# Attention, soft expert layer and gated MLP in one kernel: new order of the expert layers, w2 read in 4 KB runs, new planner durations, transposes moved into layer 2

## The chip, the cores and the metric

The kernel runs on one core of a Trainium2 chip. The metric is the time of one execution in microseconds (us); three runs of the kernel before were timed, and one more execution was profiled.

The engines are called by the profile's names: PE (TensorE matmul), PEld (its weight loads), DVE (VectorE), ACT (ScalarE), POOL (GpSimd) and SP (the engine whose queue issues nearly all transfers).

## What is computed

All tensors are f32; there are 2304 tokens of 512 features.

```python
# 1. attention: 4 batches, 8 heads of 64, 576 positions, a causal window of 64
scores = q @ k.T / 8, kept where 0 <= i - j < 64
x = softmax(scores) @ v                                # (2304, 512)
# 2. soft mixture: 8 experts with 4 slots each
logits = x @ phi                                       # (2304, 32)
slot_input = softmax(logits, over tokens).T @ x        # (32, 512)
h = relu(slot_input[e] @ w1[e])                        # layer 1, w1 (8, 512, 1024)
slot_out[e] = h @ w2[e]                                # layer 2, w2 (8, 1024, 512)
x = softmax(logits, over slots) @ slot_out             # combine weights, (2304, 512)
# 3. MLP: w_in (512, 2048), w_out (2048, 512)
out = softplus(x @ w_in) @ w_out
```

## The kernel before

**Attention.** It goes over 18 tiles of 128 tokens. A tile's work is cut into named steps: `LQ`, `LK`, `LV` load q, k, v; `S` is the scores, `T` mask and row maximum (DVE), `M` the subtraction (POOL), `E` the exponential (ACT), `PT` and `PC` the transpose and its copy, `VD` the arrangement of v (two POOL copies, the second of which reads the new v tile), `PV` the product, `RI`/`XN` the division, `XT`/`XC` the transpose of x. After every four tiles, `LG` to `SA` compute logits and fold them into a running softmax over tokens. `LW` loads one 512 KB piece of w1, `W2` one of w2; all go through SP's queue. The last two tiles of logits go another way (`LD`, `LM`, `EX`, `F`, `DD`, `D2`, `P0`, `P1`), ending with the slot inputs (`SN`, `SI`, `SC`).

**The planner.** The order of the steps on each engine is not written by hand. `arrange` takes every step's cost on each engine that may do it, its dependencies and a due time, plays a greedy schedule, and returns the steps sorted by planned start. The kernel issues them so, and each engine executes its own in that order; the costs have no other effect. A loaded tile is taken to land `LANDS` = 2.0 us after its issue slot on Q (SP's queue). There are two plans: `steps_1` for attention, `steps` for the MLP. `TILE` is the planned time per attention tile.

**Layers 1 and 2.** These are written by hand. `emit_l1(grp)` does layer 1 of four experts (64 matmul records), `emit_relu` its relu, one half on ACT, one on DVE, into two buffers that both groups use. `emit_h1t` transposes the two halves on PE (L598), each followed by two DVE copies into `hTz` (L605). `emit_l2(j)` does layer 2 for pieces of w2; an odd j makes 8 matmul records, an even one none. `emit_nat` computes the logits of the last two tiles once more in the other orientation. The softmax over slots (L632 to L647, into `lnat` and `cc`) stands in the code ahead of `emit_relu(0)`.

**The MLP.** For each of 16 feature blocks f and each of five token groups of 4, 4, 4, 3 and 3 tiles, `H` computes the hidden block, `B`, `E` (ACT) and `G` (DVE) its softplus, `GH` and `GL` split it into two parts, `Y` adds three matmuls per tile (L858 to L860) to one of four PSUM banks, and `O` takes the sum out at the end of a slab. A slab is a range of f (`SLABS`); all groups pass through one slab before the next. Weights come as raw 64-bit data (`R`), four at a time at first, and are converted by four operations each (`C`), then split (`SH`, `SL`). Ahead of the first `H` stand: `SO`, `ST`, `SE` (the layer 2 result copied, transposed, copied), `CT` and `CE` (the combine weights `cc` transposed on PE and copied to `cT`), `WD`, `PC`, `PS` (w_in multiplied by the slot output). Where the plan leaves PE idle ahead of the first `Y`, `keep_warm` fills in matmuls without use (L140).

Of the kernel before, what the change touches and what calls it, by code (L numbers as in the profile page):

```python
# [24 lines left out]
SLABS = (0, 2, 5, 10, 16)  # L25
# [9 lines left out]
ENGINES = dict(GL="PD", GH="AD", SH="AD", SL="PD", WQ="AD", PC="A", O="AD", SO="AD", SE="A", CE="AD", C="AD")  # L35
# [6 lines left out]
TILE = 4.9  # L42
# [63 lines left out]
def block_kernel(ctx: ExitStack, tc: tile.TileContext, q, k, v, phi, w1, w2, w_in, w_out, cst, out):  # L106
# [79 lines left out]
    etd = sp1.tile([NS, 256], F32, name="etd")  # L186
# [193 lines left out]

    def do_lm(e, u):
# [7 lines left out]
    def do_ex(e, u):  # L389
        nc.scalar.activation(out=etd[:, 128 * u:128 * u + 128], in_=ps_t.pop(("ld", u))[0:NS, 0:128], func=AF.Exp, bias=gn[0:NS], accum_out=sd[:, u:u + 1])  # L390
# [37 lines left out]
    def emit_nat(t, bk):  # L428
        ps = bank(bk, "nat_ps")
        for kk in range(4):  # L430
            nc.tensor.matmul(ps[:, 0:NS], xt_t[t][:, 128 * kk:128 * kk + 128], phi_sb[:, kk, :], start=kk == 0, stop=kk == 3)
        nc.scalar.copy(lnat[:, t, :], ps[:, 0:NS])
# [8 lines left out]

    extra, wpc = [], []
# [9 lines left out]
    def emit_rinv():  # L452
        nc.vector.tensor_tensor(out=s_sum, in0=s_sum, in1=f_sb, op=ALU.mult)
        ps = bank(7, "r_ps")
        for u in range(2):
# [9 lines left out]
                D2=do_d2, P0=do_p0, P1=do_p1, SN=do_sn, SI=do_si, SC=do_sc, NA=do_na, CL=do_cl, W2=do_w2)  # L465
# [15 lines left out]
    for t in range(NT + 1):  # L481
        if t < NT:
            if t:
                step_1(("LQ", t), dict(Q=0.7), [("S", t - NQB)])
                step_1(("LK", t), dict(Q=0.7), [("S", t - NKB + 1)])
                step_1(("LV", t), dict(Q=0.7), [("PV", 2 * (t - NVB) + 1), ("VD", t - NVB + 1)])
# [42 lines left out]
    step_1(("P1",), dict(E=0.6), [("P0",), ("D2",), ("XN", 17)])
    for h in range(2):  # L530
        step_1(("SN", h), dict(A=0.36, D=0.4), [("P1",)])
        step_1(("SI", h), dict(E=0.3), [("SN", h), ("EX", 1), ("D2",)])
        step_1(("SC", h), dict(A=0.2, D=0.2), [("SI", h)], goal=110.0)
    step_1(("NA",), dict(E=0.6), [("XC", 16), ("XN", 17)], goal=111.0)
    for n, js in enumerate((range(NWC0), range(NWC0, NWC0 + NWC1))):
        step_1(("CL", n), dict(Q=0.01), [("S", 17), ("LW", N1 - 1)] if n == 0 else [("PV", 35), ("CL", 0), ("VD", 17)])
        for j in js:
            step_1(("W2", j), dict(Q=1.37), [("CL", n), ("W2", j - 1)])

    with tc.manual_schedule():  # L540
# [6 lines left out]
        nc.scalar.dma_start(out=phi_sb, in_=phi.rearrange("(k p) s -> p k s", p=128))  # L547
# [17 lines left out]
        def emit_l1(grp):  # L565
            ps = [bank(2 * grp + hh, "l1_ps") for hh in range(2)]
            l1_ps[grp] = ps
            for kt in range(4):
# [439 lines left out]
```

## Time and profile before

| | us |
|---|---|
| median of 3 runs (382.62 to 384.53) | 383.97 |
| the profiled execution, its own time | 381.92 |
| its span, first to last instruction | 380.1 |
| PE busy | 363.0 (95%) |
| DVE busy | 277.9 (73%) |
| ACT busy | 238.4 (63%) |
| POOL busy | 104.4 (27%) |

The span is counted from the first instruction; 1.8 us of the execution lie outside it. Busy time of PE counts a matmul to its modelled end, and matmuls are pipelined, so the distance between starts says more than the durations. A row of a timeline has a start, a duration, the engine and the line; what stands in brackets is idle time of the engine ahead of it, and what ended it.

### The profile page before, as it was taken

How to read it: one execution, taken by the hardware profiler on the slowest of the kernel's cores; microseconds unless marked ns; L12 is line 12 of the kernel's file. 1: busy time of each engine (PE TensorE's matmuls, PEld its weight loads, DVE VectorE, ACT ScalarE, POOL GpSimd, SP SyncE). 2: the span in 40 equal slices, each digit the busy share in tenths (PEclk: the TensorE clock that was granted, in tenths of full speed). 3: DMA queues.
4: the chain of work that ended last, by engine and by line, in shares of the span. 5: the costliest groups of instructions: out<-in, count | busy, mean ns of one | idle time of the engine just before them, and what ended most of it. 6: DMA issues, size and time to landing. Idle time of an engine off the chain costs nothing.

```text
span 380.1 us, 8149 instructions
## 1 busy us (share of the span) xinstructions
PE 363.0 (95%) x3013; PEld 268.9 (71%) x3013; DVE 277.9 (73%) x780; ACT 238.4 (63%) x467; POOL 104.4 (27%) x121
## 2 busy tenths in 40 slices
PE   7799999999898999998999999999999999999995
PEld 5588778786333285776887677878866888888884
DVE  1477777765144089999899989898899986767463
ACT  1467676753121089888858789466887794656760
POOL 2687787660011001021113421011324000002230
PEclk9999999999999999999999999999999999999999
DMA  8999999999999992341112433104010002112022
GB/s 290 365 322 399 401 393 399 397 403 382 381 376 387 377 353 92 114 164 55 56 57 62 153 119 110 41 17 148 17 57 2 1 20 92 55 58 83 28 85 83
DMA packets 35192, 70.27 MB, mean 185 GB/s; under 512 B 3280, under 2 KB 11472, under 8 KB 35152
## 3 DMA queue, kind: packets, MB, share of 16 engines
q1 hardware_dynamic: 34336, 69.03, 50.3%
q10 hardware_dynamic: 816, 0.72, 0.6%
q8 instruction: 24, 0.39, 0.4%
q14 instruction: 16, 0.13, 0.1%
HBM read 65.02 MB, written 4.72 MB: 183 GB/s over the span
## 4 chain that ended last, share of the span: by engine, by line
PE 75%; DVE 12%; ACT 5%; issue 4%; POOL 2%; DMA 1%; SPq 0%; DVEq 0%; POOLq 0%; ACTq 0%
PE y_ps L858 14%; PE y_ps L859 14%; PE y_ps L860 14%; PE x_ps L269 5%; PE pt_ps L251 5%; PE s_ps L224 5%; PE l_ps L613 3%; PE x_ps L829 2%; PE xt_ps L292 2%; DVE g L841 2%; PE l_ps L572 2%; PE h_ps L829 1%; ACT a L832 1%; DVE cv L699 1%; DMA vt<-v_d 1%
## 5 line engine op out<-in xcount | busy, mean ns | idle before, releaser
L858 PE MATMUL y_ps<-whi,gh 128*128 128x512 f32 x288 | 115.3, 400 | 1.3 <-DVE part L735 0.9
L859 PE MATMUL y_ps<-wlo,gh 128*128 128x512 f32 x288 | 114.2, 397 | 0.0
L860 PE MATMUL y_ps<-whi,gl 128*128 128x512 f32 x288 | 114.1, 396 | 0.1
L738 POOL TENSOR_TENSOR gl<-g,gh 128x384 fp32r<-128x384 f32 (+2 forms) x28 | 31.7, 1131 | 177.6 <-PE x_ps L829 62.0
L858 PEld LDWEIGHTS y_ps<-whi,gh 128*128 128x128 f32 x288 | 54.1, 188 | 17.3 <-issue 2.9
L860 PEld LDWEIGHTS y_ps<-whi,gl 128*128 128x128 f32 x288 | 54.1, 188 | 14.0 <-DVE gl L738 1.4
L859 PEld LDWEIGHTS y_ps<-wlo,gh 128*128 128x128 f32 x288 | 54.1, 188 | 11.6 <-DVE wlo L738 0.3
L837 ACT ACTIVATE a<-a 128x512 f32<-128x512 f32 (+2 forms) x81 | 47.4, 585 | 2.6
L836 ACT ACTIVATE a<-a 128x512 f32<-128x512 f32 (+2 forms) x81 | 47.3, 584 | 1.3
L235 DVE CUSTOM_DVE_ANT_0 sm<-s_ps,cst_sb 128x128 f32<-128x128 f32 x144 | 32.1, 287 | 20.9 <-PE s_ps L224 20.3
L832 ACT ACTIVATE a<-x_ps 128x512 f32<-128x512 f32 (+2 forms) x50 | 27.1, 546 | 25.5 <-PE x_ps L829 21.8
L242 POOL TENSOR_TENSOR sm<-mx,sm 128x512 f32<-128x512 f32 x36 | 37.0, 1035 | 13.6 <-ACT xt L195 6.9
L738 DVE TENSOR_TENSOR gl<-g,gh 128x512 fp32r<-128x512 f32 (+1 forms) x53 | 34.1, 646 | 2.9 <-ACT gh L735 1.6
L841 DVE SCALAR_TENSOR_TENSOR g<-x_ps,a 128x512 f32<-128x512 f32 (+2 forms) x50 | 31.2, 625 | 6.0 <-ACT a L832 2.1
L245 ACT ACTIVATE sm<-sm 128x512 f32<-128x512 f32 x36 | 22.7, 634 | 16.9 <-POOL sm L242 16.9
L735 DVE CAST gh<-g 128x512 fp32r<-128x512 f32 (+2 forms) x51 | 20.0, 393 | 13.2 <-PE y_ps L859 12.7
L869 DVE TENSOR_TENSOR part<-y_ps,part 128x512 f32<-128x512 f32 x36 | 24.6, 687 | 4.1 <-PE y_ps L860 3.2
L832 ACT ACTIVATE a<-h_ps 128x512 f32<-128x512 f32 (+1 forms) x31 | 17.0, 549 | 16.2 <-PE h_ps L829 16.0
L195 ACT COPY pt<-pt_ps 128x512 f32<-128x512 f32 x35 | 19.5, 586 | 11.2 <-PE pt_ps L251 11.0
L251 PE MATMUL pt_ps<-cst_sb,sm 128*128 128x128 f32 x144 | 22.2, 290 | 3.2 <-ACT sm L245 2.4
L224 PE MATMUL s_ps<-kr,qb 64*64 64x128 f32 x576 | 23.0, 301 | 1.9 <-DMA kr<-k_d 1.9
L224 PEld LDWEIGHTS s_ps<-kr,qb 64*64 64x64 f32 x576 | 18.0, 147 | 7.8 <-issue 5.2
(144 smaller groups left out, 551.9 us busy)
## 6 DMA issues: line engine op xcount, KB each, us to landing
w1t<-w_d SPq DMA_DIRECT2D x32, 512.0 KB, 7.7
w2t<-w_d SPq DMA_DIRECT2D x29, 512.0 KB, 10.2
wi<-w_in_d SPq DMA_DIRECT2D x16, 512.0 KB, 4.9
wo<-w_out_d SPq DMA_DIRECT2D x16, 512.0 KB, 4.0
vt<-v_d SPq DMA_DIRECT2D x18, 260.0 KB, 6.6
qb<-q_d SPq DMA_DIRECT2D x18, 256.0 KB, 6.1
out_d<-o SPq DMA_DIRECT2D x18, 256.0 KB, 2.0
kr<-k_d SPq DMA_DIRECT2D x17, 256.0 KB, 6.3
```

The costliest lines, as they stand in the source:

```text
L224: nc.tensor.matmul(s_ps[2 * t + a][64 * par:64 * par + 64, 128 * p:128 * p + 128], qb[t % NQB][rows, p, 64 * par:64 * par + 64], rhs, star ...
L235: nc.vector.tensor_tensor_reduce(out=sm[:, p], in0=ps[:, 128 * p:128 * p + 128], in1=mask, scale=-0.125, scalar=3.0e38, op0=ALU.add, op1=A ...
L242: nc.gpsimd.tensor_tensor(out=sm_t[i], in0=mb, in1=sm_t[i], op=ALU.subtract)
L251: nc.tensor.transpose(ps[:, 128 * p:128 * p + 128], sm[:, p], ident)
L738: eng[e].tensor_tensor(out=dst, in0=a, in1=b.bitcast(F32), op=ALU.subtract)
L832: nc.scalar.activation(out=st["a", i], in_=st["h", i], func=AF.Abs)
L836: nc.scalar.activation(out=a, in_=a, func=AF.Exp, scale=-1.0)
L837: nc.scalar.activation(out=a, in_=a, func=AF.Ln, bias=1.0)
L841: nc.vector.scalar_tensor_tensor(out=st["g", i], in0=st["h", i], scalar=0.0, in1=st["a", i], op0=ALU.max, op1=ALU.add)
L858: nc.tensor.matmul(y, st["gh", i][:, ts], hi, start=first, stop=False)
L859: nc.tensor.matmul(y, st["gh", i][:, ts], lo, start=False, stop=False)
L860: nc.tensor.matmul(y, st["gl", i][:, ts], hi, start=False, stop=last)
```

## The change

The diff does these things.

- **w2 runs.** In a piece of w2 each partition takes two neighbouring rows (one run of 4 KB) in place of rows 128 apart (two runs of 2 KB). Layer 1's hidden units are transposed with a step of two columns to match. Three of the 32 pieces are loaded into two half tiles each and keep 2 KB runs.
- **Logits of the last two tiles.** `emit_nat` goes (twice 8 matmul records and an ACT copy). In its place `LC` copies the logits beside the exponentials, `DD` transposes both together, and `NL` copies them into `lnat`.
- **Order of the layers.** After layer 1 of group 0: its relu, the first half of layer 1 of group 1, `emit_h1t(0)`, the second half, and then the softmax over slots, with `emit_relu(1)` in the middle of it. Eight pieces of layer 2, not six, stand ahead of `emit_h1t(1)`.
- **Combine weights.** `CT` and `CE` leave the MLP's plan. The 18 transposes and 5 copies stand between pieces of layer 2, on ACT and DVE in turn.
- **First slab.** Token group 0 has one block in its first slab and four in its second.
- **Planner.** Most costs are replaced: for instance `S` 1.15 to 1.05, `PV` 0.75 to 0.6, `VD` 1.5 to 1.25, transfers 0.7 to 0.67 and 1.37 to 1.31, `TILE` 4.9 to 4.6, `Y` 0.6425 to 0.7. `SE` may go on DVE as well.
- **phi** is laid out on the host so that each partition reads one run of 512 B in place of four of 128 B.

```diff
-SLABS = (0, 2, 5, 10, 16)
+SLABS = ((0, 1, 5, 10, 16),) + ((0, 2, 5, 10, 16),) * 4
-TILE = 4.9
+TILE = 4.6
...
-        src = w2[e, 256 * r:256 * r + 256, :].rearrange("(a p) f -> p a f", p=128)
+        src = w2[e, 256 * r:256 * r + 256, :].rearrange("(p a) f -> p a f", a=2)
...
+    def do_lc(e, u):
+        evac(e, etd[NS:2 * NS, 128 * u:128 * u + 128], ps_t["ld", u][NS:2 * NS, 0:128])
...
-            nc.tensor.transpose(ps_t["dd"][:, NS * u:NS * u + NS], etd[:, 128 * u:128 * u + 128], ident[0:NS, 0:NS])
+            nc.tensor.transpose(ps_t["dd"][:, 64 * u:64 * u + 64], etd[:, 128 * u:128 * u + 128], ident[0:64, 0:64])
...
+    def do_nl(e):
+        evac(e, lnat[:, 16:18, :], ps_t.pop("dd")[:, 0:128].rearrange("p (u s) -> p u s", u=2)[:, :, NS:2 * NS])
...
-    def do_na(e):
-        emit_nat(16, 4)
...
-                step_1(("LQ", t), dict(Q=0.7), [("S", t - NQB)])
+                step_1(("LQ", t), dict(Q=0.67), [("S", t - NQB)])
...
-                    step_1(("LW", j), dict(Q=1.37), [("LW", j - 1)], goal=100.0)
+                    step_1(("LW", j), dict(Q=1.31), [("LW", j - 1)], goal=100.0)
...
-                    nc.tensor.transpose(pst[:, 128 * f:128 * f + 128], h1[hh][:, 128 * f:128 * f + 128], ident)
+                    base = h1[hh][:, 256 * (f // 2) + f % 2:256 * (f // 2) + f % 2 + 1]
+                    rows = bass.AP(tensor=base.tensor, offset=base.offset, ap=[list(base.ap[0]), [2, 128]])
+                    nc.tensor.transpose(pst[:, 128 * f:128 * f + 128], rows, ident)
...
-        emit_nat(17, 5)
         emit_rinv()
+        emit_relu(0)
+        emit_l1(1, range(2))
+        emit_h1t(0)
+        emit_l1(1, range(2, 4))
...
         nc.vector.tensor_reduce(out=cm, in_=lnat, axis=AX.X, op=ALU.add)
+        emit_relu(1)
         nc.vector.tensor_scalar_add(cm, cm, 1e-9)
...
-        emit_relu(0)
-        emit_l1(1)
-        emit_h1t(0)
-        emit_relu(1)
-        for j in range(6):
+        for j in range(8):
             emit_l2(j)
         emit_h1t(1)
...
         for j in range(NWC, N2):
             emit_l2(j)
+            b, odd_j = divmod(j - NWC - 3, 2)
+            if not odd_j and 0 <= b < 5:
+                n = min(4, NT - 4 * b)
+                ps = bank((3, 0, 7)[b % 3], "c_ps")
+                for x in range(n):
+                    nc.tensor.transpose(ps[:, 128 * x:128 * x + 128], cc_t[b][:, x].rearrange("p a s -> p (a s)").bitcast(F32), ident)
+                (nc.vector.tensor_copy if b % 2 else nc.scalar.copy)(cT[:, 512 * b:512 * b + 128 * n], ps[:, 0:128 * n])
...
-        for a, b in zip(SLABS, SLABS[1:]):
+        for n in range(len(SLABS[0]) - 1):
             for g, nt in enumerate(GROUPS):
+                a, b = SLABS[g][n:n + 2]
                 for f in range(a, b):
...
-                step(("Y", i, j), dict(E=0.6425), deps, goal=goal)
+                step(("Y", i, j), dict(E=0.7), deps, goal=goal)
...
-        ("q_d", pairs(q)), ("k_d", pairs(k)), ("v_d", vh.reshape(NTOK, 520)), ("phi_d", inputs["moe_phi"]),
+        ("q_d", pairs(q)), ("k_d", pairs(k)), ("v_d", vh.reshape(NTOK, 520)), ("phi_d", inputs["moe_phi"].reshape(4, 128, NS).transpose(1, 0, 2)),
```

## Rows read from the trace of the kernel before

**Rows 1.** Busy time by stretch: start:end, length, engines' busy time (instructions), PEclk, DMA, GB/s.
```profile
30.00:50.00 20.00, 20.00 (x418) 16.39 (x414) 14.59 (x96) 14.44 (x30) 15.66 (x20) 1.00 1.04 398
...
122.10:133.40 11.30, 11.30 (x105) 3.28 (x104) 1.48 (x5) 0.00 (x0) 0.00 (x0) 1.00 1.06 379
...
150.00:180.00 30.00, 28.88 (x133) 21.66 (x134) 29.13 (x55) 25.38 (x52) 4.98 (x4) 1.00 0.32 106
```

**Rows 2.** PE in the MLP, timeline: Y matmuls 30 starts apart, and the last one.
```profile
150.12 0.39 PE L858 MATMUL y_ps<-whi,gh 128*128 128x512 f32 x1
...
157.11 0.34 PE L829 MATMUL h_ps<-cT,wst 128*128 128x384 f32 x1
...
375.92 0.40 PE L860 MATMUL y_ps<-whi,gl 128*128 128x512 f32 x1
```

**Rows 3.** PE's other matmuls in the MLP, groups by line: shapes xcount | busy us, mean ns | idle before.
```profile
L801 PE MATMUL wq_ps<-wit,soT 128*32 128x256 f32 x56 | 4.5, 391 | 0.9 <-DVE wit L700 0.9
...
L809 PE MATMUL wp_ps<-wq,cst_sb 128*128 128x256 f32 x14 | 4.2, 378 | 0.0
```

**Rows 4.** SP's queue near the end of attention, timeline.
```profile
71.71 2.36 SPq L146 DMA_DIRECT2D w1t<-w_d  x4
75.09 0.33 SPq L206 DMA_DIRECT2D vt<-v_d  x1
```

**Rows 5.** POOL at the last attention tile, timeline.
```profile
84.33 0.61 POOL L261 COPY vd<-vt 64x520 f32<-64x520 f32 x1 [1.55 <-DMA vt<-v_d]
```

**Rows 6.** DVE and ACT between attention and layer 1, timeline.
```profile
93.99 0.16 DVE L384 TENSOR_TENSOR gn<-gn,nm 128x1 f32<-128x1 f32 x1
94.64 0.18 ACT L432 COPY lnat<-x_ps 128x32 f32<-128x32 f32 x1 [2.31 <-PE x_ps L431]
94.73 0.30 ACT L387 ACTIVATE f<-negm,gn 128x1 f32<-128x1 f32 x1
```

**Rows 7.** PE in layers 1 and 2, timeline.
```profile
99.95 7.07 PE L572 MATMUL l_ps<-w1t,siT 128*32 128x512 f32 x64 [0.30 <-ACT siT L195]
106.96 1.08 PE L431 MATMUL x_ps<-phi_sb,xt 128*128 128x32 f32 x8
108.16 7.07 PE L572 MATMUL l_ps<-w1t,siT 128*32 128x512 f32 x64
117.15 0.66 PE L598 MATMUL x_ps<-cst_sb,s_acc 128*128 128x128 f32 x4 [1.33 <-DVE hTz L605]
117.74 2.78 PE L613 MATMUL l_ps<-w2t,hTz 128*32 128x512 f32 x24
121.55 0.66 PE L598 MATMUL x_ps<-cst_sb,s_acc 128*128 128x128 f32 x4 [0.44 <-DVE hTz L605]
122.13 11.37 PE L613 MATMUL l_ps<-w2t,hTz 128*32 128x512 f32 x104
```

**Rows 8.** DVE in the softmax over slots, its later part, timeline.
```profile
111.67 0.18 DVE L636 TENSOR_SCALAR cm<-cm 128x18 f32<-128x18 f32 x1
...
116.02 0.23 DVE L646 TENSOR_TENSOR cc<-lnat,cc 128x64 fp32r<-128x64 f32 x1
```

**Rows 9.** From layer 2 to the first Y, timeline.
```profile
132.14 0.43 DVE L694 TENSOR_SCALAR cv<-wi 128x512 f32<-128x512 f32 x1 [9.61 <-DMA wi<-w_in_d]
133.43 1.09 PE L747 MATMUL c_ps<-cst_sb,cc 128*128 128x128 f32 x8
137.53 0.27 ACT L735 CAST wst<-wp_ps 128x128 fp32r<-128x128 f32 x1
142.80 0.68 DVE L738 TENSOR_TENSOR wlo<-wot,whi 128x512 fp32r<-128x512 f32 x1
143.28 0.40 PE L858 MATMUL y_ps<-whi,gh 128*128 128x512 f32 x1
```

**Rows 10.** Transfers of raw w_in, by line: KB each, median us from issue to landing.
```profile
wi<-w_in_d SPq DMA_DIRECT2D x16, 512.0 KB, 4.9
```

More of the change, by code (lines that the diff above doesn't have):

```diff
@@ L185, in block_kernel @@
     negm = [sp1.tile([128, 1], F32, name=f"negm{i}") for i in range(2)]
-    etd = sp1.tile([NS, 256], F32, name="etd")
+    etd = sp1.tile([2 * NS, 256], F32, name="etd")
     sd = sp1.tile([NS, 2], F32, name="sd")
@@ L426, in do_sc @@
         evac(e, siT[h], ps_t.pop(("si", h))[:, 0:2 * NS])
[L428 to L432, printed above, removed]
-    def do_na(e):
-        emit_nat(16, 4)
+    extra, wpc = [], []
     def open_extra(st, bufs, side, first):
@@ L503, in block_kernel @@
             x = t - 1
-            in_ring(("XT", x), 0.55, ("XC", x), dict(A=0.58, D=0.69), [("XN", x)], [("LG", (x - XTB) // 4)])
+            in_ring(("XT", x), 0.54, ("XC", x), dict(A=0.58, D=0.69), [("XN", x)], [("LG", (x - XTB) // 4)])
             if x % 4 == 3:
                 b = x // 4
-                step_1(("LG", b), dict(E=1.15), [("XC", y) for y in range(x - 3, x + 1)] + [("SA", b - 1)])
+                step_1(("LG", b), dict(E=1.05), [("XC", y) for y in range(x - 3, x + 1)] + [("SA", b - 1)])
                 step_1(("LT", b), dict(A=0.27), [("LG", b)])
@@ L546, in block_kernel @@
         nc.scalar.dma_start(out=cst_sb, in_=cst)
-        nc.scalar.dma_start(out=phi_sb, in_=phi.rearrange("(k p) s -> p k s", p=128))
+        nc.scalar.dma_start(out=phi_sb, in_=phi)
         keep_warm(14, 7)
@@ L563, in block_kernel, with emit_l1 @@
         takers += [None] * (32 - len(takers))
[L565 to L568, printed above, removed]
+        def emit_l1(grp, kts=range(4)):
+            if grp not in l1_ps:
+                l1_ps[grp] = [bank(2 * grp + hh, "l1_ps") for hh in range(2)]
+            ps = l1_ps[grp]
+            for kt in kts:
                 for hh in range(2):
@@ L648, in block_kernel @@
             cc_t.append(cc)
-        emit_relu(0)
-        emit_l1(1)
-        emit_h1t(0)
-        emit_relu(1)
-        for j in range(6):
+        for j in range(8):
             emit_l2(j)
         emit_h1t(1)
-        for j in range(6, NWC):
+        for j in range(8, NWC):
             emit_l2(j)
@@ L741, in ncol @@
             return 128 * (items[i][5] - items[i][4])
-        def do_ct(e, b):
-            ps = st["ct", b] = bank((3, 0, 7)[b % 3], "c_ps")
-            for j in range(min(4, NT - 4 * b)):
-                nc.tensor.transpose(ps[:, 128 * j:128 * j + 128], cc_t[b][:, j].rearrange("p a s -> p (a s)").bitcast(F32), ident)
-        def do_ce(e, b):
-            n = 128 * min(4, NT - 4 * b)
-            copy(e, cT[:, 512 * b:512 * b + n], st["ct", b][:, 0:n])
         def do_so(e, h):
@@ L864, in do_o @@
             y = y_t.pop((g, j))
[L865 removed]
+            if f == SLABS[g][1] - 1:
                 copy(e, part[g, j], y)
@@ L892, in block_kernel @@
             step(("SE", h), dict(A=0.26, D=0.33), [("ST", h)])
-        for b in range(5):
-            n = 128 * min(4, NT - 4 * b)
-            step(("CT", b), dict(E=n * 0.00085), [("CE", b - 3)])
-            step(("CE", b), dict(A=0.09 + n * 0.00076, D=0.066 + n / 960), [("CT", b)])
         nb = 16 - NX
@@ L911, in block_kernel @@
                 m = 2 * j + u
-                step(("SH", m), dict(A=0.58, D=0.42), [("C", "wo", j, u, 3), ("SH", m - 1)])
-                step(("SL", m), dict(P=1.25, D=0.69), [("SH", m)])
+                step(("SH", m), dict(A=0.51, D=0.34), [("C", "wo", j, u, 3), ("SH", m - 1)])
+                step(("SL", m), dict(P=1.3, D=0.61), [("SH", m)])
             elif j == 0:
@@ L932, in block_kernel @@
             o = 128 * (start[g] + ta)
-            deps = [("PS", f // 2 + 1 if f > 1 else f), ("G", i - NA)] + [("CE", x) for x in range(o // 512, (o + n - 1) // 512 + 1)]
-            step(("H", i), dict(E=n / 2400 + 0.005), deps + ([held[b]] if b in held else []))
+            deps = [("PS", f // 2 + 1 if f > 1 else f), ("G", i - NA)]
+            step(("H", i), dict(E=n / 2200), deps + ([held[b]] if b in held else []))
             held[b] = ("G", i)
-            step(("B", i), dict(A=0.14 + n * 0.0008), [("H", i)])
-            step(("E", i), dict(A=0.35 + n * 0.0016), [("B", i)])
-            step(("G", i), dict(D=0.13 + n / 960), [("E", i), ("GL", i - NG)])
-            step(("GH", i), dict(A=0.15 + n * 0.00083, D=0.13 + n / 1920), [("G", i)] + [("Y", i - NH, j) for j in range(4)])
-            step(("GL", i), dict(P=n * 0.00238, D=0.13 + n / 960), [("GH", i)])
+            step(("B", i), dict(A=0.06 + n * 0.00085), [("H", i)])
+            step(("E", i), dict(A=0.26 + n * 0.00164), [("B", i)])
+            step(("G", i), dict(D=0.07 + n / 960), [("E", i), ("GL", i - NG)])
+            step(("GH", i), dict(A=0.08 + n * 0.00085, D=0.07 + n / 1920), [("G", i)] + [("Y", i - NH, j) for j in range(4)])
+            step(("GL", i), dict(P=0.15 + n * 0.0022, D=0.07 + n / 960), [("GH", i)])
             for j in range(ta, tb):
                 deps = [("GL", i), ("SL", f), ("Y", i, j - 1)]
-                if i == 0:
-                    deps += [("CE", x) for x in range(5)]
                 if first:
```

66 lines of the change are left out of this document (33 added, 33 removed).

## The prediction

> **What bounds the kernel now.** I read the busy time by stretch first. In attention PE is busy 20.00 of 20 us while the transfers run at 398 GB/s; in layer 2 PE is busy 11.30 of 11.30 us at 379 GB/s, with DVE and ACT nearly idle; early in the MLP (150 to 180) PE is busy 28.88 and DVE 29.13 of 30 us [rows 1]. So PE sets the pace throughout, transfers stand close behind it until layer 2 ends, and DVE stands close behind it in the first part of the MLP.
>
> Then the MLP's timeline. 30 matmuls take 157.11 - 150.12 = 6.99 us, 0.233 each [rows 2]. Y needs 288 x 3 = 864 of them, 201.3 us; H goes over 16 x 2304 columns, 72 matmuls of 512 columns, 16.8 us at the same pitch (an estimate). First Y to the end of the last is 376.32 - 143.28 = 233.0 us [rows 2, 9]. That leaves 14.9 us, of which the two other matmul groups take at most their busy 4.5 + 4.2 [rows 3]; pipelined like the rest I put them at 6. So PE stalls for some 9 us in the MLP (6 to 15 at the ends).
>
> Third, the places between stages, taken up below. The sum is made against the profiled execution, 381.92 us (span 380.1 and 1.8 around it); the median of the runs shown, 383.97, lies 2.05 above it, and I add that at the end.
>
> **Attention's order.** The last v tile is issued at 75.09, behind four w1 pieces from 71.71 [rows 4], and POOL waits 1.55 us for it [rows 5]. In POOL's order the last `M` is queued behind that copy; for `M` wait the last `E`, `PT`, `PV` and the whole end of the softmax. Why four pieces stand there: by the old costs a tile takes PE 1.15 + 2 x 0.55 + 2 x 0.75 + 0.55 + (1.15 + 0.35 + 0.75)/4 = 4.86, and the queue 3 x 0.7 + 2 x 1.37 = 4.84, so two w1 pieces fit in each tile. By the new ones PE takes 1.05 + 2 x 0.5 + 2 x 0.6 + 0.54 + (1.05 + 0.3 + 1.0)/4 = 4.38, and 3 x 0.67 leave 2.37 for w1, 1.8 pieces of 1.31. Fewer pieces should stand ahead of the last v; one less is 0.524 MB at 398 GB/s [rows 1], 1.3 us. The w1 pieces pushed back have until 99.95 [rows 7]. I take the wait as gone: -1.5. Bounds: the wait and one piece, -2.9; a wait of this size at another tile, +1.6. A new order of all other steps has no row and lies within these bounds only if no tile waits twice. phi's shorter runs: 64 KB at 398 GB/s is 0.16 us at most; 0.
>
> **Logits of the last two tiles.** `F` starts at 94.73 behind an ACT copy at 94.64 that waited 2.31 us for `emit_nat`; DVE had what `F` needs at 94.15 [rows 6]. Without that copy `F` can start 0.5 us sooner: -0.5 (0 if an `LC` copy comes to stand there). `LC` and `NL` are four copies of about 0.2 us like the one at 94.64, in ACT's idle 2.31 us; 0, and 0.8 if that cover is gone.
>
> **Layers 1 and 2.** Before, 99.95 to 133.43, 33.5 us [rows 7, 9]. After, in order: layer 1 of group 0, 7.0; `emit_rinv`, 0.3 (`emit_nat`'s 0.9, from 106.96, is gone); half of layer 1, 3.5; `emit_h1t(0)`, 1.7, its price when the second half waits 0.44 for DVE (it took 2.6 here, with a wait of 1.33); half of layer 1, 3.5; 32 records of layer 2 at 11.37/104 = 0.109, 3.5; `emit_h1t(1)`, 1.7; 96 records, 10.5; 18 transposes at 1.09/8, less the pipelined end, 2.3 [rows 7 to 9]. One wait moves: DVE does its half of `emit_relu(1)` (about 0.7, like the 512-column row at 142.80) only when layer 1 ends, then the rest of the softmax over slots, 116.25 - 111.67 = 4.6 [rows 8], and only then the copies for which the second transposes of `emit_h1t(1)` wait: 5.3 + 0.3 + hand-overs of 0.2 after layer 1's end. PE gets there at 3.5 + 0.66 and would wait 0.44 anyway, so it waits 1.1 more. Sum 35.1: +1.6. Bounds: no such wait, +0.5; transposes that read with a step of two columns have no row, and at twice the 0.66 of four they add 2.6 to the 16, so +4.2. I take the plain price, as all rows of PE's operands here are for plain reads. The five copies to `cT` lie under layer 2, where ACT shows 0.00 and DVE 1.48 of 11.3 us [rows 1]; without that cover, 5 x 0.68 = 3.4.
>
> **w2 in 4 KB runs.** 29 whole pieces are 15.2 MB: 40.1 us at the 379 GB/s of w2 in 2 KB runs, 38.2 at the 398 of the mixed loads of attention [rows 1]. The first raw weights, for which DVE waits until 132.14 [rows 9], should land 1.9 us sooner (0 at the other end, if SP's queue is held up elsewhere). In the sum it counts 0: layer 2 ends after that in either case. It is the cover for DVE's work at the MLP's start.
>
> A rule speaks against this part. The Trainium skill, "DMA: Bandwidth & Descriptors", section Bandwidth, says that for loads from HBM the HBM's share of about 358 GB/s for a core binds, not the run length. By that rule the raw weights land no sooner, and the MLP's start has to absorb up to 1.9 us. The trace does not agree: 398 GB/s in attention.
>
> **Start of the MLP.** From layer 2's end to the first `Y`: 143.28 - 133.43 = 9.85 us [rows 9]. PE's first eight `CT` transposes (1.09) stand ahead of `ST`; gone. From `PC` at 137.53 to `Y` at 143.28 pass 5.75 us, at whose end PE waits for `wlo`, started on DVE at 142.80 behind the conversion of block 1. With one block in group 0's first slab, block 1 is needed by the third item, not the second, so `wlo` need not wait for it. Eight short steps like `PC` (0.27) with hand-overs are an estimate of 3.3. So at best 9.85 - 1.1 - 2.45 = 6.3; I take 7.5, two thirds of the way, since DVE and ACT are contended there: -2.35 (bounds -3.5 and 0).
>
> **The first slab itself** adds no work: 18 `O` copies and ten items stand ahead of block 2 in both orders. Group 0's four copies come sooner, into a full DVE: 0, and 4 x 0.68 = 2.7 if all delay PE.
>
> **The MLP's planner.** `Y` at 0.7 is three times the measured 0.233; the old 0.6425 was too fast. Truer costs should remove some of the 9 us of stalls. But DVE has 0.9 us free in 30 [rows 1], and PE would start 2.6 us sooner against 1.9 us from the transfers. I take -1.5, nearer to nothing than to -9; at the other end stands the rival below.
>
> **Sum.** -1.5 - 0.5 + 1.6 - 2.35 - 1.5 = -4.25: 377.7 for an execution like the profiled one, 379.7 at the median.
>
> **Rivals.** *The planner does more* (0.15): two thirds of the 9 us go, -6 in place of -1.5, and the time is 375.2. For it: DVE and PE are both a little short of full. Against: nothing removes DVE work in the MLP but one copy.
>
> *DVE takes it back* (0.2): PE starts sooner, but each conversion is due when it was, so PE waits later; the -2.35 and the -1.5 vanish: -0.4, 383.6. It decides if the raw weights land no sooner. For it: 29.13 of 30 us; against it: 398 GB/s beside 379. (The rule of the Trainium skill's "DMA: Bandwidth & Descriptors" above would bring this rival about.)
>
> *Slower, by raw weights that the plan takes to be there* (0.12): the plan lets a conversion start 1.456 + 1.0 us after its slot in the queue, the transfers take 4.9 [rows 10]. With truer and tighter costs conversions are put earlier in the in-order queues of DVE and ACT; one that waits for its piece holds `G`, `GH` and `GL` behind it, and PE. Each costs up to 4.9 - 2.5 = 2.4 us; three of the 28 later pieces give +7.2 - 4.25, 386.9 at the median, and two already undo the gain. Against: before, the only wait of this kind is the harmless one until 132.14.
>
> **How the numbers follow.** The forecast has 0.53, its own range 377 to 382. I write down 379.7. A measurement of this kernel can tell about 0.5%, 1.9 us, from no change. Faster than 382.05: the forecast nearly whole, and the first rival, plus some of the second, 0.72; within, most of the second and the ends of others, 0.17; slower, 0.11. The range 375.5 to 385.0 takes in the second rival and leaves out the far halves of the first and third.
>
> **What would show it.** Right: POOL's wait for the last v gone and layer 1 starting near 98; layer 2 ending near 133 with `emit_h1t(1)` waiting 1.5 us; over 390 GB/s in layer 2 and DVE's first conversion near 130; the first `Y` near 140.7; stalls of PE in the MLP a little fewer. Wrong: a v or k wait at other tiles, stepped transposes slower than 0.66 for four, a first `Y` near 143, or stalls after 150 above 9 us.

## The result, and the profile after

The changed kernel takes 388.48 us at the median of four runs (386.66 to 390.27), the kernel before, beside it, 383.3 (381.15 to 384.53): a ratio of 1.0136, 95% interval 1.0091 to 1.0181. It is slower by 5.2 us, where 4.25 us faster was forecast. A few executions of a kernel run over 1.5% longer at a lower mean granted clock; medians are over all executions, and the ratios leave those few out. The profiled spans are 386.7 and 380.1, 6.6 apart, and the stages share that out:

| stage of the profiled execution, us | before | forecast | after |
|---|---|---|---|
| start to layer 1 | 99.95 | -2.0 | 98.39 (-1.56) |
| layers 1 and 2, with the transposes of the combine weights after | 33.5 | +1.6 | 39.3 (+5.8) |
| end of layer 2 to first `Y` | 9.85 | -2.35 | 7.71 (-2.1) |
| first `Y` to last `Y` | 232.6 | -1.5 | 237.0 (+4.4) |

Two terms failed: the layers by 4.2 us and the MLP by 5.9. PE's timeline through the layers of the changed kernel (start, duration, shape, count, idle time ahead) shows the first:

```profile
94.25 0.61 PE L401 MATMUL dd_ps<-cst_sb,etd 64*128 64x64 f32 x2 [1.38 <-ACT etd L393]
...
98.39 9.91 PE L572 MATMUL l_ps<-w1t,siT 128*32 128x512 f32 x64 [0.30 <-ACT siT L195]
...
113.30 0.75 PE L600 MATMUL x_ps<-cst_sb,s_acc 128*128 128x128 f32 x4 [0.44 <-DVE hTz L607]
...
123.17 0.75 PE L600 MATMUL x_ps<-cst_sb,s_acc 128*128 128x128 f32 x4 [1.44 <-DVE hTz L607]
...
128.28 0.66 PE L719 MATMUL c_ps<-cst_sb,cc 128*128 128x128 f32 x4
128.86 1.06 PE L615 MATMUL l_ps<-w2t,hTz 128*32 128x512 f32 x8
...
145.40 0.50 PE L858 MATMUL y_ps<-whi,gh 128*128 128x512 f32 x1
```

The same 64 matmuls of layer 1 that took 7.07 us before [rows 7] take 9.91. The windows of the changed kernel (columns as in [rows 1]) show the granted clock in this stretch:

```profile
93.00:94.00 1.00, 0.00 (x0) 0.00 (x0) 0.45 (x2) 0.45 (x2) 0.00 (x0) 1.00 1.05 418
97.00:98.00 1.00, 1.00 (x8) 0.95 (x7) 0.15 (x2) 0.21 (x1) 0.00 (x0) 0.67 1.03 412
98.00:104.00 6.00, 5.70 (x29) 1.36 (x32) 0.00 (x0) 0.21 (x1) 0.00 (x0) 0.50 0.98 357
104.00:105.00 1.00, 1.00 (x12) 0.24 (x8) 0.00 (x0) 0.00 (x0) 0.00 (x0) 0.92 0.96 322
```

PE does nothing from 93 to 94, and from late in 97 to 104 its granted clock is 0.50, the lower of its levels (1.2 in place of 2.4 GHz). Before, the clock was 1.00 in every microsecond from 90 to 102, and `emit_nat`'s eight matmuls stood (from 93.53 to 94.61) where the hole is now.

Ahead of that, POOL's wait for the last v, and then DVE at the MLP's start:

```profile
83.36 0.61 POOL L261 COPY vd<-vt 64x520 f32<-64x520 f32 x1 [1.09 <-DMA vt<-v_d]
```

```profile
133.72 0.69 DVE L720 CAST cT<-c_ps 128x512 fp32r<-128x512 f32 x1 [2.47 <-PE c_ps L719]
134.32 0.42 DVE L696 TENSOR_SCALAR cv<-wi 128x512 f32<-128x512 f32 x1
...
141.40 0.29 DVE L748 TENSOR_TENSOR wst<-wp_ps,wst 64x128 fp32r<-64x128 f32 x1 [3.12 <-ACT wst L745]
```

The wait of [rows 5] is 1.09 in place of 1.55. Three pieces of w1 stand ahead of the last v now, one fewer, but that v is issued only 0.52 sooner, at 74.57. DVE starts to convert at 134.32 (before 132.14, [rows 9]), since a copy to `cT` that waits for PE stands ahead in its queue, and then stands 3.12 us for `PC`.

In the MLP, groups by line with the idle time ahead of each and who ended it, between first and last `Y`: `H` in the kernel before, then `Y` and `H` in the changed one:

```profile
L829 PE MATMUL x_ps<-cT,wst 128*128 128x512 f32 (+1 forms) x47 | 18.7, 399 | 0.7 <-DVE g L841 0.3 <-ACT a L832 0.3
L829 PE MATMUL h_ps<-cT,wst 128*128 128x512 f32 (+1 forms) x30 | 11.3, 377 | 0.4 <-DVE g L841 0.4
```

```profile
L858 PE MATMUL y_ps<-whi,gh 128*128 128x512 f32 x288 | 116.6, 405 | 0.9 <-ACT part L745 0.4 <-DVE part L869 0.2
...
L829 PE MATMUL x_ps<-cT,wst 128*128 128x512 f32 (+1 forms) x48 | 19.2, 400 | 3.7 <-DVE g L841 3.0 <-DVE wst L748 0.6
L829 PE MATMUL h_ps<-cT,wst 128*128 128x512 f32 (+1 forms) x30 | 11.2, 373 | 0.7 <-DVE wst L748 0.7
```

PE stood 1.1 us in all ahead of `H` (L829) before, 0.7 of it for `G` on DVE; now it stands 4.4, of which 3.0 for `G`. `GL` on DVE and on POOL shows what is new there, first of the kernel before, then of the changed one (count, shortest/median/longest ns, from when to when):

```profile
L738 DVE TENSOR_TENSOR gl<-g,gh x53: 546/683/694, 144.3 to 371.0; 128x512 fp32r<-128x512 f32 x37, 128x384 fp32r<-128x384 f32 x16
L738 POOL TENSOR_TENSOR gl<-g,gh x28: 453/1027/1514, 142.0 to 369.0; 128x384 fp32r<-128x384 f32 x17, 128x512 fp32r<-128x512 f32 x10, 128x128 fp32r<-128x128 f32 x1
```

```profile
L748 DVE TENSOR_TENSOR gl<-g,gh x73: 537/682/693, 148.4 to 377.5; 128x512 fp32r<-128x512 f32 x46, 128x384 fp32r<-128x384 f32 x27
L748 POOL TENSOR_TENSOR gl<-g,gh x8: 459/1030/1417, 145.5 to 270.5; 128x384 fp32r<-128x384 f32 x6, 128x128 fp32r<-128x128 f32 x1, 128x512 fp32r<-128x512 f32 x1
```

With the new costs (`GL` dearer on POOL, cheaper on DVE) 20 `GL` steps went from POOL to DVE.

### The profile page after: what moved, and what is told of

It reads as the page before. It is cut to its first block, busy times and chain, and to the rows that moved or that the text cites. A ratio compares the mean times of both kernels' runs of the same rounds, so it can differ in the third digit from the quotient of the medians.

```text
span 386.7 us, 8083 instructions
## 1 busy us (share of the span) xinstructions
PE 366.4 (95%) x3004; PEld 266.8 (69%) x3004; DVE 284.5 (74%) x794; ACT 244.6 (63%) x474; POOL 81.4 (21%) x101
## 4 chain that ended last, share of the span: by engine, by line
PE 62%; DVE 21%; ACT 9%; issue 5%; DMA 1%; POOL 1%; SPq 0%; DVEq 0%; ACTq 0%; POOLq 0%
PE y_ps L858 10%; PE y_ps L860 10%; PE y_ps L859 10%; PE x_ps L269 5%; PE pt_ps L251 5%; PE l_ps L572 4%; PE s_ps L224 4%; DVE g L841 4%; DVE gl L748 3%; PE l_ps L615 3%; DVE part L869 2%; PE xt_ps L292 2%; DVE cv L701 2%; ACT a L836 2%; PE x_ps L829 2%
## 5 line engine op out<-in xcount | busy, mean ns | idle before, releaser
L858 PE MATMUL y_ps<-whi,gh 128*128 128x512 f32 x288 | 116.6, 405 | 0.9 <-ACT part L745 0.4
L748 DVE TENSOR_TENSOR gl<-g,gh 128x512 fp32r<-128x512 f32 (+1 forms) x73 | 46.5, 636 | 2.9 <-DVE gh L745 0.5
L195 ACT COPY pt<-pt_ps 128x512 f32<-128x512 f32 x36 | 20.4, 588 | 10.7 <-PE pt_ps L251 10.6
L748 POOL TENSOR_TENSOR gl<-g,gh 128x384 fp32r<-128x384 f32 (+2 forms) x8 | 8.6, 1076 | 87.0 <-PE y_ps L860 31.1
L745 DVE CAST gh<-g 128x512 fp32r<-128x512 f32 (+2 forms) x52 | 21.5, 413 | 6.1 <-PE y_ps L859 3.8
L841 DVE SCALAR_TENSOR_TENSOR g<-h_ps,a 128x512 f32<-128x512 f32 (+1 forms) x31 | 19.6, 631 | 8.1 <-ACT a L837 7.6
L748 POOL TENSOR_TENSOR wlo<-wot,whi 128x512 fp32r<-128x512 f32 x7 | 9.7, 1380 | 74.5 <-ACT whi L745 74.4
```

What stands on the lines that cost most here:

```text
L748: eng[e].tensor_tensor(out=dst, in0=a, in1=b.bitcast(F32), op=ALU.subtract)
L841: nc.vector.scalar_tensor_tensor(out=st["g", i], in0=st["h", i], scalar=0.0, in1=st["a", i], op0=ALU.max, op1=ALU.add)
L858: nc.tensor.matmul(y, st["gh", i][:, ts], hi, start=first, stop=False)
```

## The experiments

**The clock.** *Filler matmuls.* Theory: the hole that `emit_nat` left ahead of `DD` brings the lower clock. Twelve matmuls without use fill it.

```diff
         logits(ps_t["ld", u], [16 + u] * 4)
+        if u:
+            keep_warm(12, 4)
```

> The changed kernel with twelve matmuls without use put on PE right behind the last logits, where emit_nat stood before. Theory 'clock': without emit_nat PE stands idle from 92.87 to 94.25 in the changed kernel, and its granted clock is 0.50 from about 98 to 104, so layer 1 of group 0 takes 9.84 us and not 7.0; with the gap filled the clock stays at 1.00, layer 1 takes 7.1, and the span shrinks by 2.5 to 3 us, from 386.7 to about 384. Rival 'operands': layer 1 is slow because of what it reads while 4 KB writes land in the same memory; then it stays near 9.8 and the time is that of the changed kernel.

Measured: 386.7 us, ratio 1.0092 [1.0067, 1.0117]. The window and layer 1 of this kernel:

```profile
98.00:104.00 6.00, 5.70 (x57) 2.00 (x60) 0.00 (x0) 0.43 (x2) 0.99 (x2) 1.00 1.04 392
```

```profile
98.80 7.07 PE L574 MATMUL l_ps<-w1t,siT 128*32 128x512 f32 x64 [0.30 <-ACT siT L195]
```

Layer 1 is back at 7.07 and the span is 2.4 us shorter; the stretch of the `Y`s stays at 237.1. So the clock is one loss, and the MLP another. The same filler in the kernel with the whole MLP plan undone (both are shown below) takes the median from 382.01 to 380.76.

*The kernel before without `emit_nat(16)`.* The logits of tile 16 in this orientation are zeros here, so that part is left out.

```diff
-        emit_nat(16, 4)
+        nc.gpsimd.memset(lnat[:, 16, :], 0.0)
```

> The kernel before with the logits of tile 16 in the second orientation left out: eight matmuls of emit_nat and their ACT copy go, POOL writes zeros in their place, so the combine weights of that tile are uniform and not the reference's. Theory 'clock': PE now idles from about 93.5 to 95.4, the granted clock falls to 0.50 for some 6 us behind it, layer 1 of group 0 takes 9 to 10 us in place of 7.07, and the time rises by 2 us although work was taken away. Rival 'operands' (or no tie to the gap): layer 1 stays at 7.07 and the time falls by 0.5.

Measured: 382.1 us over ten runs (380.72 to 388.14), ratio 0.9982 [0.9946, 1.0017]: the 2 us that the theory named can't be seen. Its profile, of the slowest of the ten, has 10.2 us at half clock from 99.1, but half clock before the hole as well, from 88.9 to 92.3. Over all profiles: of the seven kernels with the changed attention and no filler, all spend 8.4 to 9.8 us on layer 1 of group 0; of the five with filler, two take 7.0 and three 8.3 to 8.7; of the seven with the attention of the kernel before, six have the full clock there, and one (the DVE copies, below) has not. The mean clocks of single executions say the same: in all 40 of the seven kernels without filler it is at most 0.995, while 7 of the 48 with filler and 3 of the ten without `emit_nat(16)` have 0.996 or more. So the hole makes the lower clock likelier; it doesn't force it, and the lower clock comes without it too.

**Single parts of the MLP undone.** First the old costs back in the changed kernel (core of the edit; the others are the diff of the change, read backwards):

```diff
-            step(("GL", i), dict(P=0.15 + n * 0.0022, D=0.07 + n / 960), [("GH", i)])
+            step(("GL", i), dict(P=n * 0.00238, D=0.13 + n / 960), [("GH", i)])
...
-                step(("Y", i, j), dict(E=0.7), deps, goal=goal)
-                goal += 0.7
+                step(("Y", i, j), dict(E=0.6425), deps, goal=goal)
+                goal += 0.6425
```

> The changed kernel with all costs of the MLP's plan as they were before (Y 0.6425, GL on POOL 0.00238 a column, and so on); order of the layers, slab, w2 and attention's plan stay changed. Theory 'planner': the new costs made the plan leave GL on DVE (73 subtractions there in place of 53, 8 on POOL in place of 28), DVE is over 96% busy from 180 to 260, and PE waits for g; with the old costs POOL has about 31 of them again, the stretch from first to last Y goes from 237.4 back to about 233, and the time falls by 4 us. Rival 'slab': the one-block slab of group 0 is what costs; then the stretch stays at 237 and the time does not move.

Measured: 389.56 us, 1.0175 [1.0131, 1.0218]; first to last `Y` 237.2. Then the old slab:

```diff
-SLABS = ((0, 1, 5, 10, 16),) + ((0, 2, 5, 10, 16),) * 4
+SLABS = ((0, 2, 5, 10, 16),) * 5
```

> The changed kernel with the first slab of group 0 of two blocks, as before. Theory 'planner': the slab is not the cause; the stretch from first to last Y stays above 236 and first Y comes later, near 146 to 147, so the time is the same or 1 us longer. Rival 'slab': the early evacuation of group 0 is what costs; then the stretch falls to about 233 and the time by 2 to 4 us.

Measured: 389.44 us, 1.0176 [1.0137, 1.0214]; 236.9. And both at once:

> The changed kernel with both the old costs of the MLP's plan and the old first slab, so that of its MLP only CT and CE are missing from the plan of before. Theory 'head of queue': PS(0) again stands on DVE ahead of the last conversions of the first blocks, DVE idles for some 3 us for it, and the stretch from first to last Y stays near 237 us. Rival 'costs and slab together': either alone is enough to spoil the order; with both undone the stretch returns to about 233 and the time falls by 4 us.

Measured: 394.21 us, 1.0265 [1.0193, 1.0338]; 239.0, the worst so far. With the old costs `GL` is back on POOL (50 on DVE, and 52 with the old slab too), and the stretch is no shorter. Taken alone, these three seem to clear both parts. That reading was wrong: single parts in the kernel before, below, lose each by itself.

**DVE's wait at the MLP's start.** The plan is told that layer 2 ends 2.7 us later after DVE is free:

```diff
-FREE = dict(E=2.64, A=0.28, D=2.18, P=2.48, Q=0.1)
+FREE = dict(E=5.34, A=0.28, D=2.18, P=2.48, Q=0.1)
...
-L2_END, GOAL, SLACK, NEAR = 2.74, 4.0, 0.65, 0.1
+L2_END, GOAL, SLACK, NEAR = 5.44, 6.70, 0.65, 0.1
```

> The changed kernel whose MLP plan is told that PE and the end of layer 2 come 2.7 us later against DVE (FREE E 5.34, L2_END 5.44, GOAL 6.7), as its trace shows: DVE is done with the copies to cT at 134.3, layer 2 ends at 137.7, 3.3 us later, where the plan has 0.56. In the changed kernel DVE stands idle for 3.1 us (138.3 to 141.4) with PS(0) at the head of its queue. Theory 'head of queue': with this plan one w_out conversion, SH(0) and SL(0), 1.6 us of work, stand ahead of PS(0), the idle time shrinks to about 1.5, DVE's later work comes 1.6 us sooner, and the time falls by 1 to 2 us. Rival 'chance of the greedy order': each change of the plan's numbers gives another order with a stretch of 236 to 238 us from first to last Y; the time does not move.

Measured: 387.02 us, 1.009 [1.005, 1.0129]; DVE's wait for `PC` is 1.17 in place of 3.12, the stretch 235.7. A second kernel has the filler, all copies to `cT` on ACT, and the plan told 6.0 us:

> The changed kernel with the twelve matmuls behind the last logits, all five copies to cT on ACT, and the MLP's plan told that layer 2 ends 6 us later against DVE. DVE can then begin with the raw weights when they land, about 130.5, not at 134.3, and has more conversions ahead of PS(0). Theories 'clock' and 'DVE' together: 2.4 us from the clock, 1 to 3 us from DVE's earlier start, time 383 to 385, level with the kernel before. Rival 'chance of the greedy order': 386.5 as with the twelve matmuls alone.

Measured: 385.66 us, 1.0056 [1.0018, 1.0094]; 235.6. So the start numbers that the plan was left with may cost some 1.4 of the 4.4; that it isn't just another order is not shown, since a `Y` of 0.65 moves the stretch by 0.8 below. The converse, nine useless copies (4.11 us) on DVE after the first conversion of the kernel before:

```diff
             st["c", kind, j, u][k](e)
+            if (kind, j, u, k) == ("wi", 0, 0, 3):
+                for _ in range(9):
+                    nc.vector.tensor_copy(cst_sb[:, 128:640], cst_sb[:, 128:640])
```

> The kernel before with nine copies of a 512-column tile onto itself put on DVE behind the first converted w_in block, 9 x 0.34 = 3.1 us of work without use; the output is unchanged. Theory 'DVE': time that DVE loses at the MLP's start is not made good before DVE has slack, so most of it, 2 to 3 us, comes back in the time, part as a later first Y, part as a longer stretch after it. Rival 'PE': PE sets the pace of the MLP, and only the delay of the first Y counts, at most 1 us or so, with the stretch after it at 233 or shorter.

Measured: 389.9 us, 1.0159 [1.007, 1.0249]. In its profile layer 1 starts 4.8 us later and takes 9.7 us, mostly at half clock; both lie ahead of the edit, so the total says little. The stages do: end of layer 2 to first `Y` 11.7 instead of 9.85, first to last `Y` 232.6, as before. Of the 4.1 us that DVE loses at the start 1.9 come back as a later first `Y`, none in the stretch, which needs another cause.

**The whole MLP plan undone.** `CT` and `CE` are steps of the plan again, with old costs, old slab and `SE` on ACT; what stands ahead stays changed:

```diff
-SLABS = ((0, 1, 5, 10, 16),) + ((0, 2, 5, 10, 16),) * 4
+SLABS = ((0, 2, 5, 10, 16),) * 5
...
+        for b in range(5):
+            n = 128 * min(4, NT - 4 * b)
+            step(("CT", b), dict(E=n * 0.00085), [("CE", b - 3)])
+            step(("CE", b), dict(A=0.09 + n * 0.00076, D=0.066 + n / 960), [("CT", b)])
```

> The changed kernel with its whole MLP plan set back: old planner costs, old slabs, transposes and copies of the combine weights as steps of the plan again. Attention, layers 1 and 2 and the 4 KB loads of w2 stay changed. Theory A, the order of the MLP alone loses the 4.4 us between first and last Y: the stretch returns to 232.6 us (232 to 233.5), layer 2 is about 1 us shorter than in the changed kernel, first Y comes about 9.9 us after it instead of 7.7, and the profiled span is about 386.7 - 4.4 + 2.1 - 1.0 = 383.4, or 380.6 if layer 1 also gets its full clock. Theory B, something ahead of the MLP (the loads that land sooner, DVE's late start) makes the stretch longer: it stays at 236 to 237.

Measured: 382.01 us, 0.9991 [0.9956, 1.0026]; stretch 232.4, end of layer 2 to first `Y` 9.85, span 379.8. The order of the MLP alone carries its loss. `H` in this kernel:

```profile
L832 PE MATMUL x_ps<-cT,wst 128*128 128x512 f32 (+1 forms) x46 | 18.2, 396 | 0.7 <-DVE g L844 0.3 <-ACT a L835 0.2
L832 PE MATMUL h_ps<-cT,wst 128*128 128x512 f32 (+1 forms) x30 | 11.4, 379 | 0.4 <-DVE g L844 0.4
```

Only `CT` and `CE` back in the plan, new costs and slab kept:

> The changed kernel with only the transposes and copies of the combine weights moved back from layer 2 to the MLP's plan; new costs and slabs stay. Theory A1, their move is what unsettles the order: the stretch from first to last Y is 232 to 234. Theory A2, the new costs or the slab do it, each alone being enough: it stays at 236 to 238 us. In both layer 2 with its transposes is 13.8 - 1.0 = about 12.8 us, and first Y comes 1 to 2 us later after it.

Measured: 388.18 us, 1.0164 [1.0105, 1.0222]; 239.0. The last 96 records of layer 2 take 10.44 us, against 13.85 with the transposes among them, and first `Y` comes 9.52 after, against 7.71. So the move of `CT` and `CE` brought first `Y` 1.8 us nearer to layer 2's end and put that end 3.4 us back.

**One part alone in the kernel before.** The new costs of the MLP only:

> The kernel before with only the MLP's new planner costs (a Y of 0.7 instead of 0.6425, cheaper work on DVE, dearer on POOL). Theory A, they alone lose time: the plan hands 77 of 81 GL steps to DVE where before handed 53, DVE is busy over 38 of 40 us in the middle, and the stretch from first to last Y is 235 to 237, 386 us in all. Theory B, they only do harm with the other parts: 232 to 233.5, 383 us.

Measured: 386.19 us, 1.0098 [1.0066, 1.0129]; 237.0. This is 4.3 from the costs alone, nearly the whole loss of the changed kernel, with the same sign in the profile:

```profile
L829 PE MATMUL x_ps<-cT,wst 128*128 128x512 f32 (+1 forms) x47 | 18.5, 395 | 4.4 <-DVE g L841 4.4
```

```profile
L738 DVE TENSOR_TENSOR gl<-g,gh x77: 286/682/695, 142.2 to 375.5; 128x512 fp32r<-128x512 f32 x47, 128x384 fp32r<-128x384 f32 x29, 128x128 fp32r<-128x128 f32 x1
```

The costs in halves. TensorE's (`H`, `Y` and the goals, which are their due times):

> The kernel before with only TensorE's new costs in the MLP's plan (H, Y 0.7 and the goals). 60 of 81 GL on DVE. [...] If it is the engines' costs that lose: 231.5 to 233.5, 382 to 383.5.

Measured: 384.03 us, 1.0037 [1.0004, 1.0071]; 233.8, with 60 `GL` on DVE. Those of DVE, ACT and POOL:

> The kernel before with only the new costs of DVE, ACT and POOL in the MLP's plan, TensorE's as before. 71 of 81 GL on DVE. If DVE's extra steps lose the time: 235 to 238 us from first to last Y. If TensorE's costs do: 231.5 to 233.5.

Measured: 385.14 us, 1.0064 [1.0034, 1.0094]; 234.0, with 71. Neither half is the whole of it: if DVE's extra steps lost the time, 71 `GL` there should have given 235 to 238. Each half loses 1.2 to 1.3, and both together 4.3, more than their sum.

Is it DVE's load, or is the old order simply a good draw? One cost moved by a hundredth in the kernel before:

```diff
-                step(("Y", i, j), dict(E=0.6425), deps, goal=goal)
-                goal += 0.6425
+                step(("Y", i, j), dict(E=0.65), deps, goal=goal)
+                goal += 0.65
```

> The kernel before with one cost of the MLP's plan changed by a hundredth: a Y of 0.65 instead of 0.6425 us, which is neither better nor worse as a figure. The plan's order changes, 49 GL steps stay on DVE (before 53, changed kernel 73). Theory A, it is DVE's extra steps that lose the time: the stretch from first to last Y stays at 232 to 233.5. Theory B, the old order is a good draw and nearly any other is worse: 234.5 to 238, a time 2 to 5 us over the kernel before.

Measured: 381.98 us, 0.9966 [0.9925, 1.0008]; 231.8, even a little shorter, in another order with 49 `GL` on DVE. And the new slab only:

> The kernel before with only the first slab of group 0 cut to one block: 55 GL steps on DVE. Theory A (DVE's steps lose the time): 232 to 233.5 from first to last Y, 382 to 383.5 in all. Theory B (any other order loses): 234.5 to 238, 385 or more.

Measured: 390.14 us over four runs (389.19 without one of 590.91), 1.016 [1.0085, 1.0236]; 240.4, with 55. The windows of its worst stretch:

```profile
200.00:210.00 10.00, 8.91 (x43) 6.05 (x42) 10.00 (x16) 8.37 (x18) 2.71 (x2) 1.00 0.30 101
210.00:220.00 10.00, 6.89 (x31) 3.86 (x29) 9.90 (x15) 6.15 (x12) 3.82 (x3) 0.93 0.43 137
220.00:230.00 10.00, 9.92 (x35) 7.52 (x31) 7.09 (x12) 3.49 (x7) 1.29 (x1) 0.73 0.23 66
```

and PE's waits in it:

```profile
213.76 0.50 PE L859 MATMUL y_ps<-whi,gh 128*128 128x512 f32 x1 [1.12 <-DVE part L870]
...
219.07 1.08 PE L802 MATMUL wq_ps<-wit,soT 128*32 128x256 f32 x8 [1.39 <-DVE wit L700]
```

DVE is full (10.00 and 9.90 of 10), PE starves to 6.89 of 10, and then its clock goes to half for 6.8 us, which is some 3.4 of the 7.7 lost (an estimate: half of 6.8). The remaining 4.3 are as much as the costs lose alone.

**w2, and the best combination.** The old MLP plan with the filler, everything ahead of the MLP changed:

> The MLP plan of the kernel before with the changed attention, layers 1 and 2 and w2 loads, and 12 filler matmuls in TensorE's gap ahead of the transposes of the exponentials. If the gain ahead of the MLP is real and only the plan takes it back: layer 1 of about 7.0 us, the stretch at 232.6, span about 386.7 - 4.4 + 2.1 - 1.0 - 2.6 = 380.8, so 0 to 1 us over the kernel before at most. If the plan is not the cause, 384 or more.

Measured: 380.76 us, 0.9956 [0.9932, 0.998]; stretch 232.4. In this kernel w2 in 2 KB runs again, and plain transposes:

```diff
-        src = w2[e, 256 * r:256 * r + 256, :].rearrange("(p a) f -> p a f", a=2)
+        src = w2[e, 256 * r:256 * r + 256, :].rearrange("(a p) f -> p a f", p=128)
```

> The best combination so far (old MLP plan, changed attention and layers, filler matmuls) with w2 loaded in 2 KB pieces again and the transposes of h1 unstepped. If the 4 KB loads are hidden behind the order of the layers: 380 to 381.5 us, equal within 0.3%. If the loads' rate sets first Y: raw weights land 1.5 to 2 us later and it is 1 to 2 us slower, 382 to 383.

Measured: 381.53 us, 0.9951 [0.9924, 0.9978], the same. DVE's first conversion with 2 KB runs, and then with 4 KB runs in the kernel above, which differs only in these runs and transposes:

```profile
132.06 0.43 DVE L696 TENSOR_SCALAR cv<-wi 128x512 f32<-128x512 f32 x1 [9.36 <-DMA wi<-w_in_d]
```

```profile
131.00 0.43 DVE L698 TENSOR_SCALAR cv<-wi 128x512 f32<-128x512 f32 x1 [7.46 <-DMA wi<-w_in_d]
```

The raw weights land 1.1 us sooner, at 401 in place of 386 GB/s from 107 to 120, and first `Y` doesn't come sooner for it (143.44 with 4 KB, 142.58 with 2 KB).

Last, the best kernel with `Y` at 0.65:

> Old MLP plan but a Y of 0.65, changed attention, layers and w2 loads, filler matmuls. If the gains add: a stretch of 231.8 instead of 232.4, so about 380.0 us and a ratio of 0.993 to 0.996 against the kernel before. If not, 381 to 383.

Measured: 380.61 us, 0.9935 [0.9904, 0.9965] against the kernel before at 382.82: by a little it is faster than both kernels. Span 377.6, layer 1 in 7.0, stretch 231.9.

## Why the prediction was wrong

**The MLP's planner (forecast -1.5, measured +4.4): the step that failed.** "Truer costs should remove some of the 9 us of stalls" took the costs for measurements whose only effect is a better forecast. The new costs alone lengthen the stretch by 4.3 us in the kernel before, where PE then waits 4.4 us for `G` in place of 0.7. In this planner a cost chooses the engine as well as the order. The new ones made `GL` dear on POOL and cheap on DVE; 20 more went to DVE at 0.683 us, 13.7 us of work (all of DVE's busy time from first to last `Y` rises by 9.4, from 196.0 to 205.4). The prediction had the row that speaks against it, 29.13 of 30 us busy on DVE [rows 1], and used it only as a bound on the gain. Nor were there 9 us to win: the profile before has PE idle for 3.4 us of that stretch. Windows of 180 to 260, first the kernel before, then the changed kernel, then the kernel before with only the new costs:

```profile
180.00:260.00 80.00, 79.45 (x347) 61.31 (x346) 72.98 (x134) 58.43 (x107) 15.57 (x12) 1.00 0.23 73
```

```profile
180.00:260.00 80.00, 77.51 (x334) 58.56 (x333) 77.39 (x140) 62.87 (x113) 8.64 (x7) 1.00 0.30 93
```

```profile
180.00:260.00 80.00, 77.73 (x332) 57.98 (x331) 77.97 (x138) 62.47 (x111) 8.70 (x7) 1.00 0.29 91
```

POOL's work falls from 15.57 to 8.64, DVE's rises from 72.98 to 77.39, and PE gets 77.51 where it had 79.45. That the plan is the cause is shown (the whole plan undone gives 232.4), and that the costs alone are enough too (237.0). That DVE's extra `GL` are the path by which they lose is argued, from `G` as what `H` waits for, and not shown: the number of `GL` on DVE does not order the losses. 71 lose 1.3 and 60 lose 1.2, while 50 to 55 lose 4.5 to 7.7 with the slab or the move of `CT` and `CE`. No run moves `GL` and leaves the order. `Y` at 0.7 "three times the measured 0.233" is true and still cost 1.2, with `H` and the goals.

**The slab (forecast 0, at most +2.7) and the move of `CT` and `CE`** lose too, each alone: the slab +4.3 beside the clock's 3.4; with old costs and slab, the plan without `CT` and `CE` takes 239.0 against 232.4 with them (here `SE` was free to go to DVE as well). The three don't add up: all together take 237.0. For the slab DVE's full windows show where the time goes. In the plan without `CT` and `CE` PE stands 3.5 us ahead of `Y` in place of 1.3, nearly all for `O` on DVE, and 2.9 ahead of `H` in place of 1.2; why these come late, with 52 `GL` on DVE, stays open, beyond the 3.1 us that DVE stands for `PC` at its start. That any order but the old one loses is refuted by `Y` at 0.65.

**Layers 1 and 2 (forecast +1.6, measured +5.8): the second step that failed.** By its own steps: layer 1 of group 0 7.0, measured 9.84; the two `emit_h1t` with their wait 1.7 + 1.7 + 1.1, measured 1.86 + 2.86; the halves of layer 1 and 32 records 10.5, measured 10.57; 96 records and 18 transposes 12.8, measured 13.85. The wait that moves to the second `emit_h1t` is a hit: 1.44 in the trace, 1.5 foretold (the prediction's own terms, 5.8 less 4.16 and 0.44, make the extra wait 1.2 and not 1.1). The miss is the clock, 2.84. It was made in the step on the logits: I let `emit_nat`'s matmuls go from an ACT queue and counted 0.5 for it, without asking what filled PE there. The filler run, with 7.0, and the mean clocks above bear it out as a matter of odds; why the clock falls in one execution and not in another stays open. The transposes between pieces of layer 2 were priced too low by 1.0: 8 records take 1.0 there and 0.875 in a row. The stepped transposes take 0.74 to 0.75 for four instead of 0.66, near the plain price that was taken.

**Attention and logits (forecast -2.0, measured -1.56).** The size held, the path didn't, so this hit is in part luck. POOL's wait shrank by 0.46, not 1.55; `F` comes 0.29 sooner, with two `EX` now ahead of it on ACT instead of the copy; from `F` to layer 1 pass 3.95 instead of 5.22, with `DD` now ahead of `P0`; the forecast had no term for that.

**Start of the MLP (forecast 7.5, measured 7.71)** is a hit by both its terms: it takes 9.16 with the old slab and 9.52 with `CT` and `CE` in the plan. It is paid for in layer 2, as the latter run shows (3.4 us there for 1.8 here). **w2 in 4 KB runs (forecast 0)** is a hit as well, weights 1.1 us sooner of the 1.9 foretold and no gain. By the Trainium skill, "DMA: Bandwidth & Descriptors", section Bandwidth, the HBM's share of about 358 GB/s for a core binds loads from HBM, and the rate would not have risen; these traces do not agree, with 386 and 401 GB/s in the same stretch. The same section of the Trainium skill gives that share as what each core gets while both cores of an HBM domain stream, and this kernel runs on one core; the run length, which the prediction sets beside it, is the prediction's own word.

**The rivals.** None was it. "DVE takes it back" named the right engine, but its worst case was that the gain vanishes, and its condition (raw weights no sooner) didn't hold; that the new costs could make the MLP's order worse was in none. "Slower, by raw weights" had the right sign, 386.9, by a mechanism that the profile doesn't show: after 150 neither DVE nor ACT waits for a transfer.

## What to carry to other kernels

Where a greedy planner picks engines by cost, a corrected cost is a change of order and of load: before trusting it, count the steps that change engine and lay them against the engine that is already 97% busy, and try the costs alone in the old kernel. Before taking matmuls away that look useless, look at what fills TensorE around them: a hole of 1.4 us was followed by 6.8 us at half clock. Undoing one part of a change that fails can show nothing when several parts each suffice; test each part alone in the old kernel as well.

## What the runs showed of the hardware

The clock after a hole is not certain: twelve filler matmuls closed the hole of 1.38 us in every profile, and layer 1 still ran partly at half clock (0.50 granted) in three of five, for 3.4 us each. Without filler, half clock lasted 3.4 to 10.2 us in all seven profiles of the changed attention. In the one starved stretch of the MLP, PE busy 6.89 of 10 us, half clock came too, for 6.8 us. Transposes that read every second column cost 0.74 to 0.75 us for four, plain ones 0.66; the weight load of one takes 209 ns in place of 140 (the changed kernel and the one before). Four-kilobyte runs of w2 moved 401 GB/s and two-kilobyte runs 386, side by side in otherwise equal kernels.
